# More fill products of a constant tile ahead of TensorE's pieces, and some ahead of the second block

## The chip, the cores and the metric

The kernel runs on one NeuronCore of a Trainium2 chip. Its time is the device time of one execution in microseconds; of the kernel before there are three timed runs (637.77, 639.96 and 640.91 us, median 639.96) and one profiled execution of its own (638.15 us, of which the instruction span is 636.4 us).

The names of the engines are those of the profile: PE is TensorE's matmul, PEld its weight load, DVE is VectorE, ACT is ScalarE, POOL is GpSimd, and SP is SyncE, which issues nearly all of the DMAs.

## The reference

Attention with a position bias that a small network computes, and behind it a gated feed-forward layer. Four batches, eight heads, 576 positions, 64 per head; the attention's output is read as 2304 tokens of 512.

```python
# attention
scores = (1 / sqrt(64)) * (q @ k.T)                       # (4, 8, 576, 576)
psi_rel = log1p(abs(pos[:, None] - pos[None, :]))
psi_i = log1p(maximum(pos, 1))[:, None]
h = maximum((psi_rel / psi_i)[..., None] @ w1 + b1, 0)    # hidden 32
scores = scores + (h @ w2).transpose(2, 0, 1)[None]
attn = softmax(scores)                                     # 1e-9 added to the sum
x = (attn @ v).transpose(0, 2, 1, 3).reshape(2304, 512)
# feed-forward
h = x @ w_in                                               # 512 -> 2048, float64 weights
out = (h / (1 + exp(-1.702 * h))) @ w_out                  # 2048 -> 512
```

## The kernel before, in words

The work is recorded as tasks of one engine each. A planner, `plan.order()`, sets the order of all tasks of all engines from priorities (the table TURNS), estimated costs and the buffers that are free, and the tasks are then written out in that order. Each engine runs its instructions strictly in this written order and waits on semaphores for data and buffers.

PE's tasks are called pieces and are numbered in their order from 0. The kinds of piece that matter here are these:

- Bias products (L662): the ReLU outputs, made on ACT (L636) and DVE (L638), times w2. A piece has 16 or 24 float32 matmuls. ACT (L674) or DVE (L676) copies the result out of PSUM, and SP stores it to a scratch in DRAM (L683), from which it is loaded again as the bias of a unit of 128 queries (L732).
- Scores (L983): q times k for one unit, into the PSUM tile `sp`, followed by the bias add and row minimum on DVE (L992), the exponential on ACT (L1001), its scaling into two float16 halves (ACT L1030 and DVE L750) and a transposing DMA (L1086).
- Transposes of k (L845, L846) and, for the first eight units, of the exponentials (L1054, L1051).
- Attention times v (L1077 for the first eight units, L1101 later), copied into the tile `xT` (ACT L1131, DVE L750).
- First feed-forward product m1 (L1311, 24 matmuls a piece, into `hp`), with the gate behind it (ACT L1319, DVE L1325, L1340, and others), and second product m2 (L1352, 12 matmuls a piece, into `op`).

The tokens are taken in blocks of 256; the queries of the first two batches come first, those of the other two behind them. The merge of the float64 weights on DVE (L1234, L1238, L1242, L750) and ACT (L1258) runs beside all this in the first 180 us.

A fill product (L1413) multiplies a constant float16 tile, `less`, into columns 256 to 511 of the PSUM tile `hp1` (printed as hp_124), which nothing reads. A piece that is listed in the dictionary WARM gets so many fill products in front of its own instructions, in the same place of PE's queue. `less` is made by POOL in its first six microseconds, and the first fill product waits for it.

```python
nc.tensor.matmul(
    h_tiles[1][:, 256:512], lhsT=less[:, 0], rhs=less.rearrange("p z n -> p (z n)"), start=True, stop=True
)
```

The waits are derived by tile and not by column: a fill product counts as a writer of all of `hp1`, so that it waits for the last reader of `hp1`, and a later reader of `hp1` waits for it.

Of the kernel before, what the change touches and what calls it, by code (L numbers as in the profile page):

```python
# [177 lines left out]
def kernel(  # L178
# [262 lines left out]

    MAKE_AHEAD = 1
    POOL_EXP = set()
    WARM = {2: 10, 3: 10, 17: 5, 18: 9, 19: 9, 33: 4, 51: 4, 54: 5}

    WIDE, NARROW = 1152, 592
    PITCH = 704
# [962 lines left out]
    def fill(n, fn):  # L1410
        def both():
            for _ in range(n):
                nc.tensor.matmul(  # L1413
                    h_tiles[1][:, 256:512], lhsT=less[:, 0], rhs=less.rearrange("p z n -> p (z n)"), start=True, stop=True
                )
            fn()
        return both

    with tc.manual_schedule():
        plan.order()  # L1420
        pieces = [t for t in plan.seq if t["eng"] == "PE"]
        for i, n in WARM.items():
            pieces[i]["fn"] = fill(n, pieces[i]["fn"])
# [56 lines left out]
```

## Time and profile before

| | |
|---|---|
| three timed runs | 637.77, 639.96, 640.91 us |
| profiled execution | 638.15 us, span 636.4 us, mean granted clock 0.984 |
| PE busy | 587.5 us (92%), 9236 matmuls |
| PE weight load busy | 419.6 us (66%) |
| DVE busy | 534.8 us (84%) |
| ACT busy | 377.4 us (59%) |
| fill products | 56, in front of 8 pieces, the first at 6.3 us, the last at 94.8 us |

Busy shares are means over stages that differ. From about 159 us on, PE is busy nearly all the time; before that DVE and ACT are the full engines and PE has gaps. [...] In a timeline a row starts with its start and its length in microseconds, rows of equal kind are merged (x10: ten instructions), and a bracket tells how long the engine had been idle before it and what ended that.

### The profile page before, as it was taken

To read this page: it belongs to the slowest core of one execution; us is meant where nothing else is said; L and a number is where in the kernel's file an instruction comes from. 1 tells how busy PE (TensorE), PEld (TensorE's weight loads), DVE (VectorE), ACT (ScalarE), POOL (GpSimd) and SP (SyncE) were. 2 spreads that over 40 slices of the span, in tenths; PEclk is the share of its full clock that TensorE was granted. 3 is DMA by queue.
4 is the path that set the end of the run, shared out by engine and by line. 5 is a ranking of instruction groups with operands and counts; after the bars stand their busy time and mean duration, and the time that the engine had idled before them with its cause. 6 is when DMAs were issued, how large, how long until landed. Compare 5 with 4: busy or idle time off the path is not lost.

```text
span 636.4 us, 21746 instructions
## 1 busy us (share of the span) xinstructions
PE 587.5 (92%) x9236; PEld 419.6 (66%) x9236; DVE 534.8 (84%) x1446; ACT 377.4 (59%) x836; POOL 4.9 (1%) x22
## 2 busy tenths in 40 slices
PE   6867879985999999999979999999999999999997
PEld 3435546853665667767657777766777677777784
DVE  6999999999999989898878879899797685985442
ACT  7988978697796864454535457566454444542221
POOL 3000000000000000000000000000000000000000
PEclk9999999995999999999999999999999999999999
DMA  9999996789969999999999979979969390662000
GB/s 232 302 309 299 250 264 142 175 208 228 287 174 201 173 264 199 191 185 183 203 208 215 202 179 167 183 171 192 208 138 186 75 172 35 114 113 40 34 3 35
DMA packets 254490, 113.59 MB, mean 178 GB/s; under 512 B 234036, under 2 KB 234168, under 8 KB 254392
## 3 DMA queue, kind: packets, MB, share of 16 engines
q1 hardware_dynamic: 254104, 111.84, 84.1%
q8 instruction: 72, 1.18, 0.8%
q10 hardware_dynamic: 288, 0.35, 0.2%
q14 instruction: 26, 0.21, 0.1%
HBM read 52.26 MB, written 15.61 MB: 107 GB/s over the span
## 4 chain that ended last, share of the span: by engine, by line
PE 70%; DVE 14%; DMA 6%; ACT 5%; issue 2%; SPq 2%; POOL 0%; DVEq 0%; ACTq 0%; POOLq 0%
PE hp L1311 25%; PE op L1352 24%; PE hp L1101 8%; PE sp L983 6%; PE sp L662 2%; DVE wide L992 2%; DVE wide L750 2%; DMA wide<-in_k_dram 2%; ACT wide L1001 2%; DMA w<-in_k_dram 2%; PE sp L1352 2%; DVE w L750 1%; DMA wide<-in_moe_w_in_dram 1%; DVE narrow L1238 1%; DVE narrow L1242 1%
## 5 line engine op out<-in xcount | busy, mean ns | idle before, releaser
L1311 PE MATMUL hp<-xT,w 128*64 128x256 f16 x3456 | 206.0, 273 | 3.9 <-issue 3.0
L1311 PEld LDWEIGHTS <-w 128*64 128x64 f16 x3456 | 187.4, 110 | 22.5 <-issue 13.3
L1352 PE MATMUL op<-w,gT 128*64 128x512 f16 x1632 | 196.4, 382 | 0.7 <-DVE gT L1340 0.6
L1001 ACT ACTIVATE wide<-wide,sm 128x576 f32<-128x576 f32 x144 | 110.7, 770 | 66.4 <-DVE sm L992 64.4
L1352 PEld LDWEIGHTS <-gT 128*64 128x64 f16 x1728 | 98.0, 110 | 76.8 <-issue 7.0
L1319 ACT ACTIVATE th<-hp 128x256 f32<-128x256 f32 x144 | 53.9, 378 | 96.2 <-PE hp L1311 76.5
L992 DVE CUSTOM_DVE_ANT_0 wide<-sp,wide 128x576 f32<-128x576 f32 x144 | 104.9, 751 | 5.8 <-PE sp L983 3.5
L750 DVE SCALAR_TENSOR_TENSOR wide<-wide,sm,wide 128x576 f16<-128x576 f32 x128 | 102.5, 812 | 3.0 <-ACT wide L1030 2.6
L1325 DVE SCALAR_TENSOR_TENSOR th<-th,hp 128x256 f32<-128x256 f32 x144 | 59.6, 416 | 35.2 <-ACT th L1319 34.0
L983 PE MATMUL sp<-wide,narrow 64*128 64x512 f16 (+2 forms) x720 | 65.3, 319 | 13.2 <-DVE sm L992 4.2
L1340 DVE TENSOR_TENSOR gT<-th,gT 128x256 f16<-128x256 f32 x144 | 60.2, 419 | 10.2 <-ACT gT L1333 8.1
L1101 PEld LDWEIGHTS <-v 128*64 128x64 f16 x2160 | 59.1, 112 | 6.5 <-issue 3.6
L1101 PE MATMUL hp<-wide,v 128*64 128x128 f16 (+1 forms) x2160 | 61.5, 217 | 0.9 <-DVE th L1325 0.6
L983 PEld LDWEIGHTS <-narrow 64*128 64x128 f16 (+1 forms) x960 | 28.4, 97 | 50.1 <-issue 29.5
L1030 ACT ACTIVATE wide<-wide,sm 128x576 f16<-128x576 f32 x72 | 54.1, 769 | 12.2 <-DVE sm L1010 10.0
L636 ACT ACTIVATE wide<-tab,bp 128x384 f32<-128x384 f32 (+16 forms) x94 | 56.3, 655 | 0.0
L1333 ACT CAST gT<-th 128x256 f16<-128x256 f32 x71 | 28.4, 400 | 27.9 <-DVE th L1325 16.6
L662 PE MATMUL sp<-wide,pk 128*32 128x512 f32 (+24 forms) x264 | 23.1, 467 | 7.0 <-DVE sm L992 6.5
L1028 DVE TENSOR_SCALAR wide<-wide,sm 128x576 f16<-128x576 f32 x56 | 28.3, 512 | 0.3
L1001 ACT ACTIVATION_READ_ACCUMULATOR wide<-wide,sm 128x1 f32 x144 | 27.2, 189 | 0.0
L1335 DVE CAST gT<-th 128x256 f16<-128x256 f32 x73 | 20.8, 288 | 5.2 <-PE sp L1352 3.5
L662 PE MATMUL op<-wide,pk 128*32 128x79 f32 (+25 forms) x312 | 19.5, 368 | 5.1 <-ACT wide L674 2.5
(87 smaller groups left out, 470.8 us busy)
## 6 DMA issues: line engine op xcount, KB each, us to landing
wide<-scr SPq DMA_DIRECT2D x32, 576.0 KB, 5.4
scr<-narrow SPq DMA_DIRECT2D x30, 295.5 KB, 4.4
wide<-in_moe_w_out_dram SPq DMA_DIRECT2D x16, 512.0 KB, 5.2
wide<-in_moe_w_in_dram SPq DMA_DIRECT2D x16, 512.0 KB, 6.1
narrow<-in_q_dram SPq DMA_DIRECT2D x16, 256.0 KB, 4.4
out_dram<-narrow SPq DMA_DIRECT2D x15, 256.0 KB, 3.9
w<-in_v_dram SPq DMA_DIRECT2D x4, 576.0 KB, 7.1
wide<-scr SPq DMA_DIRECT2D x8, 288.0 KB, 4.9
```

Of the source, the lines that this page charges most:

```text
L636: nc.scalar.activation(out=h, in_=tv, func=ACTF.Relu, bias=bp[:, pb:pb + 1])
L662: nc.tensor.matmul(o[32 * r:32 * r + 32, x:y], lhsT=w2b, rhs=rhs, start=True, stop=True)
L750: nc.vector.scalar_tensor_tensor(out=out, in0=in0, scalar=scale, in1=in1, op0=ALU.mult, op1=ALU.subtract)
L983: nc.tensor.matmul(pair[64 * e:64 * e + m, a, cs], lhsT=qt[r, x, hp + e, q0:q0 + m], rhs=k_of(b, hp + e, y, cs)[r], start=i == 0, stop=i == 2,
L992: nc.vector.tensor_tensor_reduce(out=slot(("a32", u))[:, cs], in0=slot(("sp", u)).rearrange("p (h a) n -> p h (a n)", h=2)[:, a, 0:S], in1 ...
L1001: nc.scalar.activation(out=t, in_=t, func=ACTF.Exp, scale=-1.0, bias=sm[:, a:a + 1], accum_out=sm[:, 2 + a:3 + a])
L1030: nc.scalar.activation(out=o, in_=t, func=ACTF.Identity, scale=r)
L1101: nc.tensor.matmul(o[64 * a:64 * a + 64, po], lhsT=vt[:, x, vc:vc + 64], rhs=t[:, 9 * y + k0, po], start=kb < 0 and i == 0, stop=kb == 3 a ...
L1311: nc.tensor.matmul(p[y0:y0 + FF, :n], lhsT=wi16[:, f // 4, cc, z, w0:w0 + FF], rhs=r, start=i == 0, stop=i == 11, skip_group_check=FF < 128,)
L1325: nc.vector.scalar_tensor_tensor(out=th, in0=th, scalar=1.0, in1=slot(("hp", j, f))[:, :n], op0=ALU.add, op1=ALU.mult)
L1340: nc.vector.tensor_tensor(out=gt[:, 1, :n], in0=th, in1=gt[:, 0, :n], op=ALU.subtract)
L1352: nc.tensor.matmul(o_of(j, i)[y0:y0 + FF], lhsT=gt[:, z, 128 * i + y0:128 * i + y0 + FF], rhs=wo16[:, NF - 1 - f, y, :], start=f == 0 and ...
```

## The change

Only the dictionary WARM changes. Its keys are the numbers of PE's pieces, its values the number of fill products ahead of each.

```diff
-    WARM = {2: 10, 3: 10, 17: 5, 18: 9, 19: 9, 33: 4, 51: 4, 54: 5}
+    WARM = {2: 22, 3: 18, 7: 3, 12: 4, 15: 4, 17: 5, 18: 10, 19: 10, 31: 4, 33: 4, 51: 5, 54: 5, 86: 8, 89: 24, 90: 14, 91: 2, 95: 6}
```

That is 148 fill products in front of 17 pieces, where there were 56 in front of 8: 92 more, each a weight load and a matmul on PE. The orders of DVE, ACT, POOL and SP stay as they were, and so does the order of PE's own pieces. Three places are shown, as the difference of PE's written order with the waits of each row; a row of three points stands for further pairs of the same two fill rows, or for rows that did not change.

The first is near the start, in front of piece 3, the second set of bias products (wide_91 holds a ReLU output). Pieces 2 and 3 come to 22 and 18 fill products.

```order
 L1413 LDWEIGHTS less
 L1413 MATMUL hp_124<-less 128x256
+L1413 LDWEIGHTS less
+L1413 MATMUL hp_124<-less 128x256
...
 L662 MATMUL op<-wide_91,pk 32x47 [waits Activation_49]
 L662 MATMUL op<-wide_91,pk 32x47 [waits DVE_49]
```

Eight fill products more stand between piece 2 and the first product of piece 3; those products wait for ACT and DVE as before.

The second is around pieces 89 and 90: attention times v (v_111), then bias products into `sp`, then the scores of a unit (narrow_104 holds its q). In the trace of before these three start at 140.53, 147.64 and 152.88 us.

```order
 L1101 LDWEIGHTS v_111
 L1101 MATMUL hp_123<-wide_88,v_111 64x128
+L1413 LDWEIGHTS less
+L1413 MATMUL hp_124<-less 128x256 [waits DVE_49]
...
 L662 MATMUL sp<-wide_89,pk 32x368 [waits DVE_49]
 L662 MATMUL sp<-wide_89,pk 32x368 [waits Activation_49]
...
 L662 MATMUL sp<-wide_96,pk 32x384
+L1413 LDWEIGHTS less
+L1413 MATMUL hp_124<-less 128x256
...
 L983 LDWEIGHTS narrow_104
 L983 MATMUL sp<-wide_97,narrow_104 128x512 [waits Activation_49]
```

Now 24 fill products stand between the attention product and the bias products, where PE's queue had nothing, and 14 between the bias products and the scores. The first of the 24 waits for DVE, the last reader of `hp1`.

The third is piece 95, an m2 (gT_119) behind an m1 into `hp1`; in the trace of before the m2 starts at 161.76 us.

```order
 L1311 LDWEIGHTS w_63
 L1311 MATMUL hp_124<-xT_114,w_63 64x256
+L1413 LDWEIGHTS less
+L1413 MATMUL hp_124<-less 128x256 [waits Activation_49]
...
 L1352 LDWEIGHTS gT_119
 L1352 MATMUL op<-w_63,gT_119 64x512 [waits DVE_49]
```

Six fill products stand between the two, and the first of them waits for ACT's reading (L1319) of what the m1 in front of it wrote.

On the other engines one wait is added: the tanh on ACT (L1319) that follows piece 86 in the written order reads `hp1` and so waits for the eight fill products ahead of piece 86.

## Rows read from the trace of the kernel before

**Rows 1.** The page, part 4: chain that ended last, by engine.

```profile
PE 70%; DVE 14%; DMA 6%; ACT 5%; issue 2%; SPq 2%; POOL 0%; DVEq 0%; ACTq 0%; POOLq 0%
```

**Rows 2.** Waits of PE, whole span: total us, times, longest us.

```profile
PE sp L662 <- DVE sm L992: 6.5, 2, 5.3
PE sp L983 <- DVE sm L992: 4.2, 5, 1.5
...
PE hp L1311 <- issue: 3.0, 1, 3.0
...
PE op L662 <- ACT wide L674: 2.5, 3, 1.4
PE sp L983 <- DVE narrow L750: 2.3, 1, 2.3
```

**Rows 3.** Windows: length, busy PE, PEld, DVE, ACT, POOL, granted clock, DMA share, GB/s.

```profile
60.00:68.00 8.00, 5.49 (x64) 4.00 (x56) 8.00 (x23) 7.34 (x16) 0.00 (x0) 0.79 1.04 295
...
148.00:154.00 6.00, 3.49 (x26) 1.07 (x20) 5.16 (x11) 5.14 (x12) 0.00 (x0) 0.50 1.10 234
154.00:159.00 5.00, 5.00 (x81) 4.42 (x78) 4.35 (x13) 4.18 (x10) 0.00 (x0) 0.53 1.05 278
```

**Rows 4.** Timeline, start of the span, PE and ACT.

```profile
6.33 2.31 PE L1413 MATMUL hp<-less 128*128 128x256 f16 x10
...
9.75 2.24 PE L662 MATMUL op<-wide,pk 128*32 128x15 f32 x20 [0.38 <-ACT wide L636]
...
12.16 0.73 ACT L674 ACTIVATE narrow<-op,ips 128x591 f32<-128x591 f32 x1
...
15.08 2.06 PE L662 MATMUL op<-wide,pk 128*32 128x47 f32 x19 [0.55 <-DVE wide L638]
...
19.15 0.75 ACT L674 ACTIVATE wide<-sp,ips 128x591 f32<-128x591 f32 x1 [0.61 <-PE sp L662]
```

**Rows 5.** Timeline of PE, 27 to 43 us.

```profile
27.12 0.66 PE L845 MATMUL sp<-idn,w 128*128 128x128 f32 x4
...
28.49 1.21 PE L662 MATMUL op<-wide,pk 128*32 128x127 f32 x24
...
41.50 1.16 PE L1413 MATMUL hp<-less 128*128 128x256 f16 x9
```

**Rows 6.** Timeline, 63 to 68 us, PE and ACT.

```profile
63.48 1.09 PE L845 MATMUL sp<-idn,w 128*128 128x128 f32 x4 [2.51 <-DMA w<-in_k_dram]
...
65.99 1.47 PE L662 MATMUL op<-wide,pk 128*32 128x255 f32 x24
...
67.54 0.75 ACT L674 ACTIVATE narrow<-op,ips 128x591 f32<-128x591 f32 x1 [0.31 <-PE op L662]
```

**Rows 7.** Timeline, 147 to 162 us, PE, ACT and DVE.

```profile
147.64 2.73 PE L662 MATMUL sp<-wide,pk 128*32 128x368 f32 x16 [5.26 <-DVE sm L992]
...
149.00 0.61 ACT L1258 ACTIVATE w<-narrow 128x512 f16<-128x512 f32 x1
...
150.47 0.90 ACT L674 ACTIVATE narrow<-sp,ips 128x224 f32<-128x224 f32 x2 [0.85 <-PE sp L662]
...
152.88 1.62 PE L983 MATMUL sp<-wide,narrow 64*128 64x512 f16 x12 [2.51 <-ACT narrow L674]
...
161.51 0.68 DVE L750 SCALAR_TENSOR_TENSOR w<-narrow,w 128x512 f16<-128x512 f32 x1
```

**Rows 8.** Timeline of PE, same kinds of piece elsewhere.

```profile
130.61 1.36 PE L662 MATMUL sp<-wide,pk 128*32 128x336 f32 x16
...
135.93 0.91 PE L983 MATMUL sp<-wide,narrow 64*128 64x512 f16 x12
...
168.87 2.78 PE L1352 MATMUL op<-w,gT 128*64 128x512 f16 x24
```

**Rows 9.** Timeline of PE near 332 us.

```profile
332.20 4.52 PE L1352 MATMUL op<-w,gT 128*64 128x512 f16 x24
```

**Rows 10.** The page, part 3: DMA queue, packets, MB, share.

```profile
q8 instruction: 72, 1.18, 0.8%
```

## The prediction

> **What bounds the kernel now.** I read the chain that ended last first, then what PE waits for, then the granted clock by windows, and only then the timelines of the places where the change puts its fill products. The chain by engine [rows 1] gives PE 70% and DVE 14%: over the whole span PE sets the end, and a gap or a slow stretch of PE counts where PE or the engine that it feeds is on that chain. PE's waits [rows 2] then say where its gaps are: 5.3 us in one piece ahead of bias products (L662, waiting for DVE), up to 1.5 us ahead of scores, 2.3 us once ahead of scores, up to 1.4 us ahead of early bias products, and 3.0 us put down to "issue", that is, to nothing that the profile shows. The reader is to see that four of these five are waits for DVE or ACT: what PE does in the meantime costs nothing, as long as it is done in time.
>
> The windows [rows 3] show what the gaps do to the clock. [...] In front of both falls PE had stood still: 2.51 us before the products at 63.48 us [rows 6], 5.26 us before those at 147.64 us [rows 7]. So there are two things to gain, and both are of the clock and not of the gaps themselves.
>
> The start needs care. The clock column has no fall there, yet ten fill products at 6.33 us took 2.31 us [rows 4], 0.231 us each, while nine at 41.50 us took 1.16 us [rows 5], 0.129 us each. Likewise a piece of bias products took 2.24 us at 9.75 us and 2.06 us at 15.08 us [rows 4], and 1.21 us at 28.49 us [rows 5]. By the durations PE starts at the lower level too, and rises somewhere between 15 and 27 us.
>
> **The change part by part.** It adds 92 pairs of weight load and matmul to PE's queue and moves nothing else. At 0.129 us a pair that is 11.9 us of work, at 0.231 us it would be 21.3 us. What counts is which of it lies in a gap.
>
> *Pieces 89, 90, 91 and 95 (142 to 163 us).* The 24 fill products take 24 x 0.129 = 3.1 us in a gap of 5.26 us, the 14 take 1.8 us in a gap of 2.51 us [rows 7]. They are covered by DVE (the row minimum that the bias products wait for) and ACT (the copy, L674, that the scores wait for). If the clock stays up, the bias products at 147.64 us, of 368 and 384 columns, take 1.36 us (336 and 352 columns at 130.61 us [rows 8]) x 376/344 = 1.49 us instead of 2.73, and end 1.24 us earlier. The copy on ACT had waited 0.85 us for them. It can't start before L1258 ends at 149.00 + 0.61 = 149.61 us, against 150.47 us [rows 7], so 0.82 us of the 1.24 get through. Two copies later the scores start 0.82 us earlier and take 0.91 us [rows 8] instead of 1.62 [rows 7], 0.71 us less. Together 1.53 us at the point where DVE takes up the scores. PE itself would gain more: its 3.49 + 5.00 = 8.49 busy us in the two windows [rows 3] would halve, 4.2 us. But the m2 piece near 162 us waits for a weight that DVE writes at 161.51 us (L750, to 162.19 [rows 7]), behind the same DVE queue, and that comes only 1.5 us earlier. The two fill products of piece 91 (0.3 us) and the six of piece 95 (0.8 us, behind a wait for ACT's tanh) lie on PE inside this difference and cost nothing; without that cover they cost their 1.1 us and the wait. Behind 162 us PE is nearly always busy, and what it has gained there it keeps. The term is -1.5 us; its ends are -4.2 us (all of PE's gain gets through) and +1.0 us: were the clock low all the same, 38 products x 0.231 = 8.8 us would stand in gaps of 7.8 us.
>
> *Piece 31 (63 us).* Four fill products, 0.5 us, lie in a gap of 2.51 us that ends with a DMA of k. If the clock then holds, the transposes take the 28.49 - 27.12 = 1.37 us that they take in [rows 5] instead of 65.99 - 63.48 = 2.51, and the bias products 1.21 instead of 1.47: 1.40 us of PE [rows 6]. But DVE is busy 8.00 of the 8.00 us here and ACT 7.34 [rows 3], and ACT waited only 0.31 us for those products [rows 6]. So little of the 1.40 can be used: I take -0.4 us, near ACT's wait, with ends of -1.4 and 0.
>
> *Pieces 2 and 3 (the start).* Twelve more products at 0.231 us are 2.8 us. The bias products behind them had waited for ACT until 9.75 us; now PE is free for them at 6.33 + 22 x 0.231 = 11.4 us, 1.7 us later. At the lower level they end at 13.7 us, and the copy on ACT, at 12.16 us before, is 1.5 us late; at the higher one (1.21 us) it is 0.5 us late. ACT has 0.61 us to give: it waits that long for PE at 19.15 us [rows 4]. Against the delay stands that denser work early should raise the clock earlier, so that the products at 15.08 us take 1.21 us, 0.85 less, and this wait of 0.61 us goes. I put the two against each other: 0, with ends of -0.6 us (the wait goes, no delay) and +2.1 us (worked out below).
>
> *The rest.* Pieces 7, 12 and 15 (3, 4 and 4 products, about 0.5 us each) stand ahead of waits of up to 1.4 us for ACT and 2.3 us for DVE, the eight of piece 86 (1.0 us) ahead of one of up to 1.5 us [rows 2]; the tanh on ACT that now waits for those eight is not reached before they are over, if they start where PE's gap starts. One product more at 18, 19 and 51 is 0.13 us each in a gap. Zero, or 0.4 us if the last three stand in the way.
>
> Sum: -1.5 - 0.4 + 0 + 0 = -1.9 us. On the profiled execution, 638.15 us with a span of 636.4, that is 636.2 us. This execution is 1.8 us faster than the median of the three timed runs, and the four lie 3.1 us apart. I set the sum against their mean, 639.2 us: 637.3 us, which is 0.4% under the median of 639.96.
>
> **The rivals.**
>
> *The fill products don't hold the clock in most executions.* The spread of 3.1 us over four executions of one program speaks for a clock, or a wait, that falls differently from one to the next, and counts that fit one execution need not fit another; after the 24 products some 2.2 us of standing still are left, close to the 2.51 us in front of the fall at 63 us [rows 6]. Then the gain of 1.9 us comes seldom, and the time is about 639.2 us. [...] If the counts fitted every second execution, the sum would be -1.0 us and the time 638.2 us.
>
> *The long "issue" wait moves.* PE's 3.0 us of "issue" [rows 2] end at 332 us, and the m2 behind takes 4.52 us [rows 9] where the same 24 matmuls take 2.78 [rows 8]: 3.0 + 1.7 = 4.7 us. The page counts 72 transfers of instructions, 1.18 MB [rows 10]; over twice 9236 PE instructions that is 64 bytes each and 256 in a transfer. The 184 added instructions shift every such boundary by 0.7 of a transfer. If the wait is a transfer that came late, which I infer and no row proves, it needn't come there again: 637.3 - 4.7 = 632.6 us. Against it: it is one wait in 72 transfers, and another may take its place.
>
> *The fill products run at the lower level and stand in the way (slower).* If the clock is still low when the 18 products of piece 3 begin, PE is through with piece 2's products at 13.7 us and reaches piece 3's at 13.7 + 18 x 0.231 = 17.8 us, against 15.08: 2.7 us late, of which ACT's 0.61 us is free, 2.1 us. With the +1.0 us of the gaps at 142 to 153 us that makes 639.2 + 3.1 = 642.3 us. It decides whether each of the 18 takes 0.231 or 0.129 us. Against it: in the trace of before the level was up by 27 us [rows 5] with less in PE's queue.
>
> **How the numbers follow.** Forecast 637.3 us, chance 0.47, its own range 635.5 to 639; no hold of the clock, 639.2 us, 0.18; the long wait goes, 632.6 us, 0.17; slower, 642.3 us, 0.18. What can be told from no change is 0.5%, 3.2 us. Below 636.8 us lie a third of the forecast (0.16), nearly all of the vanished wait (0.16) and a little of the rest: faster 0.34. Above 643.2 us lies about half of the slower case and a new late transfer: slower 0.10. The remaining 0.56 is no change. The range is 633.0 to 642.0 us: it leaves out about 1 in 10 on either side.
>
> **What would show it.** The clock in a window 148 to 159 us at or near 1.00, bias products near 147 us at 1.5 us and scores at 0.9 us, the row minimum on DVE behind them about 1.5 us earlier, and the m2 near 162 us still waiting for DVE: the first term. Fill products ahead of piece 3 at 0.129 us, and ACT's copy of the first products under 0.6 us later: the third. Products at 63 us at 1.2 us with DVE as late as before: the second. The forecast is wrong if the clock is at 0.50 behind the 24 products, if PE's later attention and m1 pieces carry their whole gain past 162 us, or if an "issue" wait of several us comes or goes.

## The result and the profile after

The changed kernel took 633.71 us (median of 5 runs, 632.26 to 634.13) against 639.53 us before (5 runs, 637.77 to 640.91): a ratio of 0.9905, 95% interval 0.9882 to 0.9927. That is faster by about 0.95%, 5.8 us. In a later series of 12 runs against 30 the ratio was 0.9941 (0.9915 to 0.9966). Single executions of one kernel lie up to 8.5 us apart there, so this text rests on the ratios for times and on traces for places. The profiled execution after took 632.81 us, span 631.0, against 638.15 and 636.4.

The chain that ended last, by engine, beside [rows 1]:

```profile
PE 72%; DVE 11%; ACT 8%; DMA 6%; issue 2%; POOL 0%; SPq 0%; ACTq 0%; DVEq 0%; POOLq 0%
```

PE has 2 points more of it and DVE 3 fewer. PE's waits over the whole span (in total, times, longest), beside [rows 2]:

```profile
PE sp L662 <- DVE sm L992: 4.6, 2, 2.5
...
PE sp L983 <- DVE narrow L750: 2.7, 1, 2.7
...
PE hp L1101 <- issue: 2.0, 2, 1.8
...
PE sp L983 <- DMA narrow<-narrow: 1.5, 1, 1.5
```

The wait of 5.3 us ahead of the bias products is 2.5 us now, since fill products stand in it. The 3.0 us of "issue" inside m1 (L1311) are not in this list any more; instead there are 2.0 us of "issue" in the x products of L1101, 1.8 us of them in one piece.

Windows of the changed kernel, columns as in [rows 3]:

```profile
38.00:41.00 3.00, 3.00 (x33) 1.27 (x30) 2.86 (x7) 0.33 (x1) 0.00 (x0) 0.50 0.77 210
60.00:68.00 8.00, 5.97 (x86) 3.65 (x80) 7.97 (x23) 8.00 (x19) 0.00 (x0) 1.00 1.01 276
148.00:154.00 6.00, 4.81 (x64) 2.84 (x66) 5.90 (x12) 6.00 (x15) 0.00 (x0) 1.00 1.14 230
154.00:159.00 5.00, 4.57 (x105) 3.93 (x100) 4.87 (x14) 5.00 (x12) 0.00 (x0) 1.00 1.17 219
256.00:320.00 64.00, 62.03 (x1022) 44.53 (x1020) 58.18 (x161) 33.33 (x77) 0.00 (x0) 1.00 1.10 194
320.00:380.00 60.00, 56.38 (x1186) 41.71 (x1182) 50.50 (x147) 31.66 (x72) 0.00 (x0) 1.00 1.04 202
```

The granted clock, which the profile gives as a share of TensorE's full one, is 1.00 at 60 to 68 us (0.79 before) and 1.00 at 148 to 159 us (0.50 and 0.53). In windows of 1 us from 5 to 200 us both traces have 1.00 or 0.50, and a value between the two only at the ends of a stretch at 0.50: these are the two levels of the prediction. But there is a new stretch at the lower level, 0.50 at 38 to 41 us, where the trace of before has 1.00:

```profile
38.00:41.00 3.00, 2.72 (x52) 1.54 (x49) 2.86 (x6) 2.51 (x6) 0.00 (x0) 1.00 0.88 252
```

A second one, 0.57 at 82 to 86 us, is not in the trace of before either; of the other traces only that of e11 has it. The pieces near 150 us, beside [rows 7] (start, duration, engine):

```profile
148.04 1.47 PE L662 MATMUL sp<-wide,pk 128*32 128x368 f32 x16 [2.54 <-DVE sm L992]
...
149.40 0.61 ACT L1258 ACTIVATE w<-narrow 128x512 f16<-128x512 f32 x1
149.91 0.88 ACT L674 ACTIVATE narrow<-sp,ips 128x224 f32<-128x224 f32 x2
...
152.30 0.91 PE L983 MATMUL sp<-wide,narrow 64*128 64x512 f16 x12 [1.16 <-ACT narrow L674]
...
160.17 0.68 DVE L750 SCALAR_TENSOR_TENSOR w<-narrow,w 128x512 f16<-128x512 f32 x1
```

The bias products take 1.47 us (2.73 before), ACT's copy starts 0.56 us earlier, the scores take 0.91 us (1.62 before). DVE's write of the weight that m2 waits for starts at 160.17 us instead of 161.51, 1.34 us earlier. At 146 us the same DVE instructions were still 0.40 us later than before. So the gaps from 142 to 163 us brought 1.74 us.

That is less than a third of the 5.34 us by which this trace ends earlier. I followed the start of the same matmul in both traces, counted from the end: against its time in the kernel before it is 1.35 us earlier at 170 and at 259 us, 3.82 at 320, 8.02 at 345, 5.34 at 380 us and from there to the end. Most of the gain comes up between 259 and 380 us, where the change adds no product at all. Two windows of the kernel before for that stretch:

```profile
256.00:320.00 64.00, 60.14 (x996) 43.15 (x994) 56.09 (x157) 31.46 (x73) 0.00 (x0) 1.00 1.16 191
320.00:380.00 60.00, 56.16 (x1154) 43.85 (x1141) 48.55 (x137) 28.86 (x66) 0.00 (x0) 0.97 1.02 207
```

Of 124 us PE is busy 60.14 + 56.16 = 116.30 before and 62.03 + 56.38 = 118.41 after, and the clock of the second stretch is 0.97 before and 1.00 after. The stretch of the 3.0 us wait itself, before (timeline of PE):

```profile
327.71 1.37 PE L1311 MATMUL hp<-xT,w 128*64 128x256 f16 x21
332.06 0.38 PE L1311 MATMUL hp<-xT,w 128*64 128x256 f16 x3 [2.98 <-issue]
```

PE stops inside one m1 piece, after 21 of its 24 matmuls, for 2.98 us. The changed kernel has such a stop inside a piece of x products, after 73 of 120:

```profile
357.44 1.33 PE L1101 MATMUL hp<-wide,v 128*64 128x64 f16 x73
360.54 0.92 PE L1101 MATMUL hp<-wide,v 128*64 128x64 f16 x47 [1.77 <-issue]
```

The profile names nothing that ended these two waits. DMA queues of the kernel before at 328 to 331 us (packets, MB, share):

```profile
q8 instruction: 1, 0.02, 3.9%
```

One packet of 0.02 MB on the queue of instructions falls into this wait: it runs from 328.70 to 330.59 us, and PE goes on at 332.06. Then I counted PE's weight loads and matmuls in their order, as the trace has them, one of each for every product. The matmul behind the 2.98 us is number 8604, those behind the two largest waits of the changed kernel are numbers 9628 and 10140. All three leave 156 when divided by 256. So do the places of all 25 waits of PE of 0.4 us or more that are put down to "issue" in the fourteen traces of this study. So these waits stand at the boundaries of blocks of 256 instructions, and the packets tell what is waited for. Each boundary has its packet, in order, the first one number 412. At the 25 waits PE goes on 1.3 to 1.8 us after the packet of the boundary has ended; of the 1006 boundaries in the fourteen traces it passes none sooner than 1.05 us after that, and half of them over 6 us after. The page of the changed kernel counts 73 packets and 1.20 MB on this queue, 16 KB each.

### The profile page after: what moved, and what is told of

Same layout as the page of the kernel before. It is cut to its first block, busy times and chain, and to the rows that moved or that the text cites. A ratio compares the mean times of both kernels' runs of the same rounds, so it can differ in the third digit from the quotient of the medians.

```text
span 631.0 us, 21930 instructions
## 1 busy us (share of the span) xinstructions
PE 590.9 (94%) x9328; PEld 422.5 (67%) x9328; DVE 534.3 (85%) x1446; ACT 377.4 (60%) x836; POOL 4.9 (1%) x22
## 4 chain that ended last, share of the span: by engine, by line
PE 72%; DVE 11%; ACT 8%; DMA 6%; issue 2%; POOL 0%; SPq 0%; ACTq 0%; DVEq 0%; POOLq 0%
PE hp L1311 27%; PE op L1352 25%; PE hp L1101 8%; PE sp L983 7%; ACT wide L636 3%; DVE wide L992 2%; PE sp L662 2%; DMA wide<-in_moe_w_in_dram 2%; ACT wide L1001 2%; PE sp L1352 2%; DVE wide L750 1%; DMA narrow<-in_q_dram 1%; DVE narrow L1242 1%; DVE w L750 1%; DVE narrow L1238 1%
## 5 line engine op out<-in xcount | busy, mean ns | idle before, releaser
L1311 PE MATMUL hp<-xT,w 128*64 128x256 f16 x3456 | 204.9, 273 | 1.9 <-DVE xT L750 1.4
L1311 PEld LDWEIGHTS <-w 128*64 128x64 f16 x3456 | 186.7, 110 | 20.3 <-issue 10.9
L1352 PEld LDWEIGHTS <-gT 128*64 128x64 f16 x1728 | 95.6, 110 | 77.6 <-issue 8.2
L1319 ACT ACTIVATE th<-hp 128x256 f32<-128x256 f32 x144 | 54.3, 379 | 88.8 <-PE hp L1311 74.6
L1101 PEld LDWEIGHTS <-v 128*64 128x64 f16 x2160 | 57.8, 111 | 7.4 <-issue 4.7
L1101 PE MATMUL hp<-wide,v 128*64 128x128 f16 (+1 forms) x2160 | 60.2, 214 | 2.0 <-issue 2.0
L662 PE MATMUL sp<-wide,pk 128*32 128x512 f32 (+24 forms) x264 | 20.9, 431 | 4.9 <-DVE sm L992 4.6
L1008 DVE TENSOR_SCALAR sm<-sm 128x1 f32<-128x1 f32 (+1 forms) x128 | 18.9, 151 | 5.8 <-ACT wide L1001 5.3
```

The lines of the kernel that those rows point to most:

```text
L1101: nc.tensor.matmul(o[64 * a:64 * a + 64, po], lhsT=vt[:, x, vc:vc + 64], rhs=t[:, 9 * y + k0, po], start=kb < 0 and i == 0, stop=kb == 3 a ...
L1311: nc.tensor.matmul(p[y0:y0 + FF, :n], lhsT=wi16[:, f // 4, cc, z, w0:w0 + FF], rhs=r, start=i == 0, stop=i == 11, skip_group_check=FF < 128,)
L1319: nc.scalar.activation(out=slot(("th", j, f))[:, :n], in_=slot(("hp", j, f))[:, :n], func=ACTF.Tanh, scale=0.851 / (XS * WIS))
L1352: nc.tensor.matmul(o_of(j, i)[y0:y0 + FF], lhsT=gt[:, z, 128 * i + y0:128 * i + y0 + FF], rhs=wo16[:, NF - 1 - f, y, :], start=f == 0 and ...
```

## The experiments

Theory A: of the gain, what comes after 164 us comes from the number of instructions that the change adds. It adds 184, which moves every boundary of 256 to another place in the program. Theory B: it comes from the clock and the lead that the fill products buy. The runs separate the products from the count: fill products are split in two halves of 128 columns (same columns, two instructions more), or products of one column and 32 rows are added in the gap ahead of piece 89 (two instructions each, almost no columns).

| run | fills | instructions more | median us | ratio to before, 95% |
|---|---|---|---|---|
| e9 | as before | 256 | 637.21 | 0.9996 (0.9970 to 1.0023) |
| e10 | second part | 256 | 636.48 | 0.9991 (0.9965 to 1.0017) |
| e1 | all | 256 | 635.46 | 0.9977 (0.9962 to 0.9993) |
| e2 | as before | 184 | 634.20 | 0.9953 (0.9938 to 0.9968) |
| e3 | first part | 184 | 634.15 | 0.9960 (0.9944 to 0.9977) |
| e4 | second part | 184 | 633.09 | 0.9948 (0.9931 to 0.9965) |
| e12 | second part, again | 184 | 634.31 | 0.9950 (0.9927 to 0.9972) |
| e5 | all (changed kernel) | 184 | 632.91 | 0.9941 (0.9915 to 0.9966) |
| e8 | second part, piece 15 | 184 | 633.14 | 0.9933 (0.9910 to 0.9956) |
| e6 | second part | 108 | 634.42 | 0.9946 (0.9925 to 0.9967) |
| e7 | second part | 224 | 633.84 | 0.9965 (0.9940 to 0.9990) |
| e11 | second part, piece 15 | 224 | 633.47 | 0.9943 (0.9914 to 0.9972) |

Each row has 12 runs, but e2 has 11 and e8 has 7. The kernel before took 636.84 us beside e1 to e4, 637.73 beside e5 to e8 (on another chip) and 637.38 beside e9 to e12. The expectations of e1 to e4 are in us and start from the 639.5 us of the first series, so I give them as ratios to that as well.

**e1, all fills, old boundaries.** 256 more instructions put the boundaries back to where they were.

```
+    HALF = {89: 24, 90: 12}
...
+                for a, b in ((0, 128), (128, 256)) if x < half else ((0, 256),):
```

> All fills of the changed kernel, but 36 of the 38 ahead of pieces 89 and 90 are split into two products of 128 columns each: the same columns, 72 more instructions on TensorE, so that from piece 91 on the stream is 256 instructions longer than before instead of 184. Theory A (of the 5.8 us gained, about 4 come from where the transfers of TensorE's instructions, 256 at a time, fall): the wait of 3 us inside m1 near 328 us is back, the two new waits of 0.6 and 1.8 us at 349 to 361 us are gone, and the time is 636.5 to 638.5 us. Theory B (the whole gain comes from the clock and from the earlier arrival that the fills buy): no such wait, 633 to 634.5 us.

Measured 635.46 us, 1.0 us under A's interval and 1.0 us above B's. As a ratio to 639.5 us A's interval is 0.995 to 0.998 and B's 0.990 to 0.992; 0.9977 lies in A's. In its trace PE stops after 21 of 24 matmuls of the same m1 piece as before, for half as long:

```profile
326.51 1.37 PE L1312 MATMUL hp<-xT,w 128*64 128x256 f16 x21
329.32 0.38 PE L1312 MATMUL hp<-xT,w 128*64 128x256 f16 x3 [1.44 <-issue]
```

But a wait of 1.21 us in the x products was there too, against A's word that both new waits would be gone.

**e2, the shift alone.**

```
+    TINY = {89: 92}
...
+                nc.tensor.matmul(h_tiles[1][0:32, 256:257], lhsT=less[:, 0, 0:32], rhs=less[:, 0, 0:1], start=True, stop=True)
```

> The table of the kernel before, and ahead of piece 89, in the gap of 5.3 us, 92 products of one column on 32 rows: 184 instructions and almost no columns. From piece 89 on the instruction stream is shifted as in the changed kernel. Theory A: 635 to 636.5 us (639.5 less 4), without the 3 us wait near 329 us and with waits of 0.6 and 1.8 us near 350 to 361 us; if the small products hold the clock at 148 to 159 us, which the granted clock there tells, 1.7 us less. Theory B: 639 to 640 us.

Measured 634.20 us, 0.8 us under A's interval; as a ratio 0.9953 is at the upper end of A's (0.993 to 0.995), and B's (0.999 to 1.001) falls. Windows of e2:

```profile
148.00:154.00 6.00, 3.49 (x42) 1.81 (x36) 4.57 (x10) 4.59 (x11) 0.00 (x0) 0.50 1.04 258
154.00:159.00 5.00, 5.00 (x82) 4.18 (x80) 4.91 (x13) 4.46 (x10) 0.00 (x0) 0.68 1.13 283
256.00:320.00 64.00, 61.97 (x992) 43.44 (x990) 57.33 (x158) 32.65 (x75) 0.00 (x0) 0.97 1.10 192
320.00:380.00 60.00, 57.26 (x1210) 42.94 (x1208) 50.96 (x148) 32.46 (x74) 0.00 (x0) 1.00 1.04 204
```

The products of one column do nothing for the clock at 148 to 159 us, it is 0.50 and 0.68, and DVE's lead moves by 0.02 us there. Yet PE is busy 119.23 of the 124 us behind 256 us, where before had 116.30.

**e9, the control of the shift.** The same small products, but 128 of them.

```
+    TINY = {89: 128}
```

> The control of the shift: the table of before and 128 products of one column ahead of piece 89 instead of 92, so that the stream behind them is 256 instructions longer and its transfers of 256 begin at the same places of the program as before. Theory A (the places decide): the time of the kernel before, ratio 0.998 to 1.002. The rival, that the small products themselves gave the 2.6 us of the run with the shift alone: ratio 0.994 to 0.997, as there.

A ratio of 0.9996: the gain of e2 is gone with 36 small products more. Windows of e9, then its timeline of PE:

```profile
256.00:320.00 64.00, 60.72 (x1006) 43.86 (x1002) 56.16 (x157) 31.34 (x73) 0.00 (x0) 1.00 1.15 192
320.00:380.00 60.00, 56.04 (x1146) 43.97 (x1144) 49.50 (x141) 29.50 (x67) 0.00 (x0) 0.97 1.04 207
```

```profile
327.46 1.37 PE L1312 MATMUL hp<-xT,w 128*64 128x256 f16 x21
331.48 0.58 PE L1312 MATMUL hp<-xT,w 128*64 128x256 f16 x3 [2.65 <-issue]
```

PE's busy time (116.76 us in both windows, 116.30 before) and clock (1.00 and 0.97) are those of the kernel before again, and it stops at the same matmul, after 21 of 24. Theory A is shown by this pair: 184 more instructions or 256, with the same fills, are 0.4% apart (0.9953 and 0.9996). Two more pairs with equal fills point the same way, e12 and e10 (0.9950 and 0.9991) and e5 and e1 (0.9941 and 0.9977).

**e3, the first part alone, and e4, the second part alone, at 184.**

```
e3:  WARM = {2: 22, 3: 18, 7: 3, 12: 4, 15: 4, 17: 5, 18: 10, 19: 10, 31: 4, 33: 4, 51: 5, 54: 5};  TINY = {89: 54}
e4:  WARM = {2: 10, 3: 10, 17: 5, 18: 9, 19: 9, 33: 4, 51: 4, 54: 5, 86: 8, 89: 24, 90: 14, 91: 2, 95: 6};  HALF = {89: 24, 90: 14}
```

> The changed table's entries for pieces 2 to 54 and none behind them, with 54 products of one column ahead of piece 89, so that the stream from there on is shifted by 184 instructions as in the changed kernel. From the two traces the first part gave 0.6 us at the start, lost 2.0 at 38 us and gave 0.8 at 63 us: plus 0.4. Theory A: 635.5 to 637 us (639.5 plus 0.4 less 4; 1.7 less where the clock holds at 148 to 159 us). Theory B: 639.5 to 640.5 us.

> The table of before for pieces 2 to 54 with the changed table's entries for pieces 86 to 95; all 38 fills ahead of pieces 89 and 90 are split in two, which makes the shift 184 instructions from piece 91 on. Theory A: 633 to 634.2 us (639.5 less 1.7 less 4), level with the changed kernel or a little below it, since the fall of the clock at 38 us stays out. Theory B, where the gain hangs on the lead that all fills give together: 633.5 to 638 us; above 636.5 the early fills carry the gain.

Measured 634.15 us for e3, level with e2's 634.20: the first part's fills are worth nothing that can be told. It missed A's interval by 1.4 us and B's by more. As a ratio 0.9960 is at the upper end of A's (0.994 to 0.996), so the miss comes from the 639.5 us. The plus 0.4 us in it, which I had read out of two traces, is not the change's all the same. e4's 633.09 us lies in A's interval, but the ratio 0.9948 does not lie in A's (0.990 to 0.992): against the kernel before beside it, it gained 3.3 us and not the 5.7 that A had added up. So the fit in us is luck. Its repeat e12 came out at 634.31 us, 0.9950 as expected.

> The second part alone at a shift of 184 once more, beside the other three on the same chip: ratio 0.993 to 0.997 as in its first run (0.9948). It is the row against which the two runs at other shifts are read.

The early windows of e3 (first line) and of e4 (the two behind) show what that 0.4 was:

```profile
60.00:68.00 8.00, 5.68 (x60) 3.86 (x51) 7.66 (x21) 7.13 (x15) 0.00 (x0) 0.79 1.00 271
```

```profile
38.00:41.00 3.00, 3.00 (x32) 1.35 (x32) 2.86 (x6) 0.29 (x1) 0.00 (x0) 0.50 0.76 226
60.00:68.00 8.00, 5.70 (x86) 3.62 (x82) 7.94 (x25) 7.94 (x18) 0.00 (x0) 1.00 0.99 249
```

e4 has no fill ahead of piece 31 and the clock is 1.00 at 60 to 68 us; e3 has the four and it is 0.79. And e4 has the old fills up to piece 54, but falls to 0.50 at 38 us just like the changed kernel. There PE stands behind DVE (3.3 us in e4, 2.7 in the changed kernel), and DVE behind a load of weights. DVE's wait in e4, 30 to 45 us:

```profile
DVE narrow L1235 <- DMA wide<-in_moe_w_in_dram: 1.8, 1, 1.8
```

It is 1.8 us here, 0.8 before, none in e2. Of the eight traces whose instructions up to piece 54 are those of before, six have a granted clock of 0.69 or less at 38 to 41 us. So the fall is not the change's: it comes in some executions and not in others, and did not come in the one trace of before. (Neither the load nor the length of the gap tells every fall: in e7 and e5 PE stood only 1.7 and 1.8 us there, and in the kernel before 2.3 us without a fall.)

**e5, the changed kernel again.**

> The changed kernel itself, beside the others on this chip, where the kernel before took 636.8 us in the runs so far. If the parts add up (shift alone -2.6, second part with the shift -3.7, all fills at the old bounds -1.4, first part nothing): 632.5 to 633.5 us. If the first part and the second help each other: under 632.5.

632.91 us, inside the interval for parts that add up, though on another chip than the parts ran on; the ratio, 0.9941, is within 0.001 of e4's and e12's.

**e10, the second part at the old boundaries.**

```
     WARM as e4;  HALF = {89: 24, 90: 14}
+    TINY = {89: 36}
```

> The second part's fills alone, halved ahead of pieces 89 and 90, with 36 products of one column: 256 instructions more, the old places. It measures the term that I forecast at 1.5 us and that the traces show as 1.5 to 2.0 us at 162 us. Theory A: that alone is left, 1.2 to 2.0 us under the kernel before (ratio 0.9965 to 0.998), and 1 to 3 us above the same fills at a shift of 184. If the lead of the fills is what brings the later gain: ratio 0.993 to 0.995, level with the shift of 184.

The ratio, 0.9991 (0.9965 to 1.0017), is 0.0011 to 0.0026 higher than A's numbers, though its interval holds them; it rules out the 0.993 to 0.995. Against e12, the same fills at 184, it is 2.2 us longer, as A had said. So the fills from 142 to 163 us alone make no difference that can be measured, though the clock mostly holds (0.72 at 148 to 154 us, 1.00 behind). Windows of e10:

```profile
148.00:154.00 6.00, 5.68 (x58) 3.82 (x58) 5.76 (x14) 6.00 (x15) 0.00 (x0) 0.72 1.11 245
154.00:159.00 5.00, 4.92 (x114) 4.19 (x114) 5.00 (x14) 4.83 (x12) 0.00 (x0) 1.00 1.13 278
...
320.00:380.00 60.00, 56.12 (x1144) 43.90 (x1140) 50.07 (x142) 29.53 (x68) 0.00 (x0) 0.97 0.98 202
```

**e6 and e7, other counts.** e6 is e4 without halves, e7 is e4 with 20 small products more.

> The old entries for pieces 2 to 54 and the changed table's for pieces 86 to 95, no fill split: the stream behind them is 108 instructions longer than before. Theory A (where the transfers of 256 instructions fall decides some 2.5 us): the fills' 1.4 us stay, and the rest depends on a new set of places: 632 to 636 us, more than 0.7 us from the 633.1 of the same fills at 184, with its waits inside m1 and the x products at places other than 328 and 358 us. Theory B (the count is nothing): 633.1 +- 0.4 us.

> As the run with the second part alone, with 20 products of one column more ahead of piece 89: 224 instructions instead of 184, so the transfers fall 40 instructions earlier in the program than there. Theory A: 631.5 to 636 us, and the waits of 1 to 2 us at 328 and 358 us of that run change in place or size. Theory B: 633.1 +- 0.4 us.

634.42 and 633.84 us: both are outside B's interval and inside the long one of A, but on another chip than the 633.1 us that B started from. Both ratios lie inside what e4 and e12 leave open, so these two don't tell A from B. In their traces the waits stand at 156 past a multiple of 256 again, and so at other products: 2.1 us in e6 after 111 of the 120 x products that stopped after 73 at 184, 1.2 us in e7 in an m2 piece. (Of the two waits that e7's expectation names in e4, the one near 328 us is not there: e4 has 0.5 us at 350 and 1.8 us at 361 us.)

**e8, fourteen fills ahead of piece 15.**

```
-    WARM = {2: 10, 3: 10, 17: 5, ...
+    WARM = {2: 10, 3: 10, 15: 14, 17: 5, ...
```

Beside e4, only the 24 fills ahead of piece 89 are halved, which keeps the count at 184.

> The second part alone with 14 fills ahead of piece 15, where in three of five traces TensorE stood for 2.7 to 3.3 us at 35 us behind a DVE that waited for a load of weights, and the granted clock was 0.50 from 38 to 41 us; the shift stays 184. If that fall is what costs 2 us in such executions and none in the others: the granted clock at 38 to 41 us is 1.00 whatever the wait, the median is 0.5 to 1.5 us under the second part alone (632 us) and the runs spread less. If the time is lost to the load itself and not to the clock: 633.1 +- 0.4 us.

633.14 us in 7 runs, with the least spread of the four kernels run beside each other (631.33 to 634.74). The clock is 1.00 at 38 to 41 us as expected. Whether the 0.5 to 1.5 us are there is left open: in us e8 is level with the 633.1 us, on another chip; its ratio is 0.0015 under e4's and 0.0008 under e5's, less than the intervals can tell. e8 is 3.18 us ahead of before at 259 us, 1.65 us more than e2, and at 380 us it is level with e2 (5.20 and 5.15). Its windows at 38 to 41 and 256 to 320 us, and a wait of PE for a DMA between 256 and 320 us in which part of the lead goes:

```profile
38.00:41.00 3.00, 2.73 (x48) 1.63 (x41) 2.86 (x6) 2.45 (x6) 0.00 (x0) 1.00 0.97 344
...
256.00:320.00 64.00, 61.45 (x988) 43.77 (x986) 56.18 (x156) 32.70 (x76) 0.00 (x0) 0.97 1.07 191
```

```profile
PE sp L984 <- DMA narrow<-narrow: 2.3, 1, 2.3
```

**e11, the candidate.** e8 with 20 small products ahead of piece 89.

> The candidate: second part, 14 fills ahead of piece 15, shift 224, whose one trace so far had no wait of over 1 us at 349 to 361 us and the shortest span, 628.4 us. If that wait stays away: ratio 0.988 to 0.992, about 1 us under the changed kernel. If the place of the waits is drawn anew in each execution: ratio 0.992 to 0.995, level with the same fills at a shift of 184.

0.9943: level with the others, and in its trace waits of 1.9, 1.0 and 0.5 us are at the boundaries. A version that beats the changed kernel was not found.

## Why the prediction was right or wrong

The time came inside the range, but not by the way that I held likeliest. The point, 637.3 us, is 3.6 us too high; I gave no change 0.56 and faster 0.34. The rival "the long issue wait moves", 632.6 us with a chance of 0.17, is what happened in the main. That the measured time lies so close to it is in part luck: the 5 runs of the first series gave a ratio of 0.9905, the 12 of the later one 0.9941, 3.8 us.

*"It adds 92 pairs ... and moves nothing else"*, with a sum of 0 for the rest, is the step that failed. The 184 instructions move the boundaries of 256 for all of the program behind them. The three kernels at 256 have a mean ratio of 0.9988, the six at 184 one of 0.9948: 0.4%, 2.5 us.

*The price of that rival* was half of the account. Starts of the same matmul, counted from the end, against the trace of before, in us:

| | added | 259 us | 320 us | 345 us | 380 us |
|---|---|---|---|---|---|
| changed kernel | 184 | -1.35 | -3.82 | -8.02 | -5.34 |
| e2 | 184 | -1.53 | -2.38 | -7.98 | -5.15 |
| e3 | 184 | -0.72 | -3.43 | -7.89 | -5.22 |
| e4 | 184 | -1.33 | -3.43 | -7.49 | -4.71 |
| e5 | 184 | -2.38 | -3.26 | -8.33 | -5.45 |
| e8 | 184 | -3.18 | -3.26 | -7.27 | -5.20 |
| e12 | 184 | +0.94 | -1.76 | -6.60 | -3.96 |
| e1 | 256 | -1.09 | -1.46 | -4.42 | -3.65 |
| e9 | 256 | -0.03 | -0.78 | -0.81 | -0.96 |
| e10 | 256 | -0.85 | -1.29 | -1.27 | -1.60 |
| e6 | 108 | -1.78 | -3.10 | -8.07 | -3.38 |
| e7 | 224 | -2.57 | -3.87 | -7.90 | -7.93 |
| e11 | 224 | -1.86 | -2.36 | -3.64 | -2.24 |

From 320 to 345 us, with the wait of 2.98 us and the slow m2 behind it, the seven traces at 184 gain 4.6 us in the mean; I had priced that at 4.7. What I left out: from 345 to 380 us, where the new waits of 0.2 to 2.0 us lie, they lose 2.65 again. And from 259 to 320 us they gain 1.7. Net 3.6 us. The same sums over e1, e9, e10 and the kernel before itself, the four with the old boundaries, are -0.7, +0.1 and -0.4, net 1.1 us in the mean. The difference, 2.6 us before rounding, agrees with the ratios. (Behind 380 us only e5 moves, by another 0.8 us back.) The places alone don't settle how long a wait is: e7 and e11 have the same count behind 163 us, and at the same matmul PE waits 1.2 us in e7 and 1.9 in e11; e7 has no wait of 0.4 us behind that and keeps all of its gain, e11 has two and ends 5.7 us later. In the stretch from 259 to 320 us DVE, ACT and PE wait for DMAs (in the kernel before DVE 2.3 us for a load of k at 262 us, ACT 3.3 us for one of q, PE 2.2 us in two waits; in the changed one DVE none for k, ACT 3.1 us in two waits, PE 1.5 us). Why those waits are other ones with 184 instructions more is not shown.

*Pieces 89 to 95*: the mechanism was right in the main. In all ten traces that have these fills the granted clock is 0.72 to 1.00 at 148 to 154 us and 0.94 to 1.00 behind, and DVE gained 1.5 to 2.0 us from 146 to 164 us, against my 1.5; m2 near 162 us waited for DVE as I said: its third matmul starts at 162.25 us before and 160.90 after, 0.06 and 0.05 us behind the end of DVE's write. Without them it gained 0.0 in e2, 0.1 in e9 and 0.4 in e3. Of the terms, the copy on ACT gained 0.96 us once the 0.40 us of delay is taken off, against 0.82 (the two starts that the prediction subtracts give 0.86), and the scores their 0.71. What fell is *"what it has gained there it keeps"*. The seven traces at 184 lie 4.1 us apart at 259 us and 1.5 us apart at 380: e8, 3.18 us ahead, gains 0.1 us from 259 to 320 us, and e12, 0.94 late, gains 2.7. In these traces those that come early to the DMAs of that stretch wait longer, and three of them lose the clock as well: e2, e5 and e8 wait 2.0 to 2.3 us for a DMA near 279 us, the granted clock is 0.50 from 280 to 283 us (0.97 from 256 to 320 us, 1.00 in the other four), and they gain 0.1 to 0.9 us in the stretch; the other four wait 1.5 us or less, keep the clock and gain 2.1 to 2.7. In times, e4 and e12 against e2 (0.9948 and 0.9950 against 0.9953) and e10 against e9 (0.9991 against 0.9996) leave 0.2 to 0.3 us of the 1.5; the intervals, 0.2% either way, leave open whether it is nothing or all. All fills together do give something at the old boundaries: e1's interval, 0.9962 to 0.9993, leaves out 1. Which of them, is open.

*Piece 31*: 0.7 us earlier in the changed trace against my 0.4, but its fills are not the cause, as e3 and e4 show. The clock is: in eight of the nine traces with 1.00 at 60 to 68 us DVE gains 0.65 to 0.66 us from 63 to 75 us, five of them without these fills; in the four with 0.79 to 0.87 it gains at most 0.2.

*Pieces 2 and 3*: the 0 was right for the fills. The changed trace by itself shows my end of -0.6 us: the bias products at 15 us take 1.19 us instead of 2.06 (those at 10.90 us take 1.24 already, against 2.24 at 9.75 us before), ACT's wait of 0.61 us is gone, and DVE is 0.62 us early at 30 us. But DVE is 0.70 us early there in e2 and e4 too, which have the old fills; e3 is level with e2 in time.

*The rival "the fills don't hold the clock"* is half right for pieces 89 and 90. Some 2.5 us of standing still were left ahead of the bias products in the changed trace, and in five of the ten traces the clock falls to 0.50 once between 147 and 155 us (means of 0.72 to 0.79 at 148 to 154 us). But it is up again by 155 us, and DVE gains 1.5 to 1.7 us there against 1.7 to 2.0 in the other five. *The slower rival* did not come: the 18 products ahead of piece 3 took 2.14 us, 0.119 us each, and the first part costs nothing that can be told.

## What to carry to other kernels

Here 184 added instructions moved every boundary of 256 behind them, and that was worth 0.4% (0.9948 against 0.9988), more than what the change was about. So time a change that adds or removes instructions against a control that has the same number of instructions and none of the effect, and one that shifts by a whole block. Before an early gain is added to the end, look for a later stretch in which the engines wait for DMAs: here a lead of 3.2 us came out of it no bigger than one of 1.5.

## What the runs showed that I had not expected

In these traces a wait of PE of 0.4 us or more that is put down to "issue" stands at a fixed instruction number: 156 past a multiple of 256, 25 times in 25. It lasts 0.4 to 3.4 us and ends 1.3 to 1.8 us after a packet of 16 KB on the queue of instructions, and all 25 lie behind 320 us, though the page counts 73 such packets. All 25 stand at the end of a block of 256 that PE runs through in 2.8 to 4.6 us, the wait left out, where the other blocks take 8.2 us in the median; 22 other blocks as short pass without such a wait. And the packet starts 1.0 to 4.1 us after PE has passed the boundary before, against 0.7 us in the median of the other blocks. So PE waited where a short block met a packet that started late. The shift changed which blocks are short: the block that ends in the wait of the kernel before takes 3.05 us, in the changed kernel the two blocks that end at 322 and 329 us take 5.2 and 6.6 and have no such wait, and those that end at 350 and 361 us, with the waits, take 3.9 and 4.4. What holds a packet up is not shown. In the three traces with one of 2.65 us or more the granted clock from 320 to 380 us averages 0.97, as it does in e6 with one of 2.08 us; in the other ten, with waits of 2.04 us and less, it is 1.00.

Executions of one program differed by up to 8.5 us, and early falls of the clock came in some and not in others (0.69 or less at 38 to 41 us in six of eight traces with the same instructions up to there). One trace of each kernel would have given the change a loss of 2 us there that it doesn't cause.
